# A gated mix of memory attention and a ReGLU network on one core: wq in row halves, ratios by GpSimd copies, another cut of the last tile, and a new order for late loads

## The chip, the cores and the metric

The kernel runs on one core of one Trainium2 chip. The metric is the device time of one execution in microseconds (us), from launch to end, the median of several runs. Engine names as in the profile: PE is TensorE (matmuls; PEld its weight loads), DVE is VectorE, ACT is ScalarE, POOL is GpSimd, SP is SyncE, which issues nearly all DMAs here.

## The reference

x is 2048 tokens by 512, in bfloat16. The output is `g * a + (1 - g) * b`, with one gate per token.

```python
g = _sigmoid((x * gate_w).sum(-1, keepdims=True))
# a: 32 heads of 16, 4 segments of 512 tokens
for s in range(N):
    logits = einsum('bhqd,bhkd->bhqk', qs, ks) * scale + mask     # causal within the segment
    a_dot = einsum('bhqk,bhkd->bhqd', softmax(logits), vs)
    num = einsum('bhld,bhde->bhle', phi(qs), M)                   # phi(t) = t + 1 if t > 0 else exp(t)
    den = einsum('bhld,bhd->bhl', phi(qs), z)[..., None] + 1e-06
    o = sig(beta) * num / den + (1 - sig(beta)) * a_dot
    M = M + einsum('bhld,bhle->bhde', phi(ks), vs)
    z = z + phi(ks).sum over tokens
a = o @ wo
# b: ReGLU with 1792 hidden columns
b = (relu(x @ W_gate) * (x @ W_up)) @ W_down
```

`q`, `k` and `v` are `x @ wq`, `x @ wk` and `x @ wv`.

## The kernel before

The work is cut into four segments of 512 tokens. For each, PE makes Q and K (heads on partitions, tokens on columns) and V, then for each of four groups of eight heads the scores, whose exponentials ACT writes to `E` tiles and POOL masks (L874, `affine_select`), then the product with V (PV, L896). DVE normalises that product (L927 to L932), turns it into `oT` (L908) and adds the recall from the memory of earlier segments (L912, L988). The network of the segment runs beside this: gate and up products, `rgr` on ACT (L1047), `hT` on DVE (L1053). The end of a segment is four output tiles of 128 tokens (`out_tile`), in which the down product of `hT` and the product of `oT` with `wo` accumulate in one PSUM bank; DVE scales it (L1075) and SP stores it. The very last tile is done in two halves of 256 columns.

PSUM has eight banks. Each product takes a bank and holds it until DVE or ACT has evicted it. So a late eviction holds up a later product on PE.

**Order.** All engines run lists that are fixed when the program is built. A planner, `Plan`, gets every piece of work as a task with an engine, a cost, dependences and a key, and lays the tasks out in time; the order in which it starts them becomes each engine's list. `LANDS` tells it when the first loads arrive, the last numbers in `plan.add` are the latencies it reckons with, and the table `SHIFT` moves the keys of some 1220 tasks one by one. At run time nothing of this is looked at: every engine runs its list in order and waits on semaphores. Where a load arrives later than planned, the engine that reads it waits, and with it all that stands behind in its list.

**PE's three modes.** Projections and the network use the whole array (`full`, L663) or, next to PV work, the same product as four column tiles of 32 (L667). Scores use row tiles (L823, L836), PV, denominators and memory use column tiles (L896, L952, L1002).

**The start.** Six dummy matmuls (L1090) come first. x of segment 0 comes as four tiles `xn` and is turned on PE (L699) into `xT[0]`; other segments are turned by a DMA (`load_xT`). The loads of weights go out in this order on SP: wq in two halves with the x tiles between (`load_q`), wk, wv, gate and up weights in pieces, down weights, wo. A half of wq is 256 of its 512 output columns, 512 bytes per row of wq. In `proj_q` the first two column groups of segment 0 are made in two halves of 256 tokens, and need only the first half of wq.

**Token gates.** `gate_tasks` multiplies `xn` with `gate_w` (L610, four per segment), and takes an exponential (L616), `rcol`. PE has no need of it, but three readers have: `ngcol` (L620, L621) scales the output, and the ratios in another layout scale the attention (`grc`, L653) and the recall. For segments 1 to 3 that layout comes from DMAs through DRAM (`ratio`, `rtok`, `rq`, `rr`; L637 to L648). For segment 0 it comes from a matmul with a fold of the identity:

```python
nc.vector.tensor_tensor(q0[:], rcol..., quad..., ALU.mult)          # L626
nc.tensor.matmul(bank(sl)[:, 0:16], lhsT=fold..., rhs=q0...)        # L629
nc.vector.tensor_tensor(grc..., src()..., gcat..., ALU.mult)        # L653
```

There is one buffer `xn`. The load for the next segment (`load_xn`, L480) waits for the four products of the segment before, and its own four products wait for it.

Of the kernel before, what the change touches and what calls it, by code (L numbers as in the profile page):

```python
# [35 lines left out]
    0: -25684, 1: 1407, 2: -1330, 3: -22978, 4: -30607, 6: 36389, 7: -5637, 8: -6641, 9:  # L36
    -9156, 10: 6383, 11: -4187, 12: -13726, 13: 12497, 14: 57538, 15: -5422, 16: 1476, 17:
    -21591, 18: 23771, 19: -4129, 20: -7981, 21: 280, 22: 7068, 25: -318, 28: 21268, 29:
    -15341, 30: -57736, 31: -21028, 32: -2196, 33: -8016, 34: -783, 35: -1107, 36: -633, 38:
    15, 40: 42372, 41: 65840, 42: 5113, 43: -71216, 44: 19414, 45: 21758, 47: 5746, 50: 654,  # L40
    51: 20403, 52: 53629, 53: -20631, 54: 7059, 55: -21405, 56: -13895, 57: -740, 58: -5913,
    59: -13897, 60: 1353, 61: -40120, 62: 24385, 63: -14621, 65: 25112, 66: 3543, 67: -38939,
    69: 6399, 71: -26793, 72: -4691, 73: -2524, 75: 40537, 76: -4748, 77: -586, 80: -1662, 81:
    -105183, 82: -62163, 83: -64288, 84: 18468, 85: -40339, 86: 37103, 87: -37065, 89: 8422,
    90: 16643, 91: -13637, 92: -14487, 93: -5073, 94: 1505, 96: -1554, 97: -747, 98: -9522,
    99: -4680, 100: 4639, 101: -97803, 102: 16395, 103: 38252, 104: -69147, 105: -10415, 106:
    27259, 107: -31419, 108: 13377, 109: -123574, 111: -12785, 112: -2378, 113: 3673, 114:
    -29140, 115: 4266, 116: -62363, 117: 88, 119: -4261, 121: -33231, 122: 9814, 123: 2110,
    125: 19178, 126: 17796, 127: -23382, 128: -6689, 129: -747, 130: 22411, 131: -31402, 132:
    -16511, 133: -1373, 134: -1496, 135: 8763, 136: 29491, 137: -749, 138: 29552, 139: -20100,  # L50
    140: 44658, 141: -80409, 142: -3139, 143: -26909, 144: 1803, 145: 386, 146: 16247, 147:
    65537, 148: -3529, 149: -6241, 150: 65653, 151: 46999, 153: 14030, 154: 44020, 155: 14760,
    156: 43561, 157: -7096, 158: 45936, 159: -26024, 160: 23457, 161: 50979, 162: -46625, 163:
    -54482, 164: 88981, 165: -28687, 166: -9744, 167: 114272, 168: -31967, 169: 9267, 170:
    38917, 171: -13229, 172: 5693, 173: -28492, 174: 3768, 177: 340, 178: -26186, 179: -31211,
    181: -31531, 182: 39351, 183: -15341, 184: -100921, 185: 22252, 186: -1779, 187: -3708,
    189: -4467, 191: 37936, 192: -46874, 193: 73026, 194: -5245, 196: 16791, 197: 4743, 198:
    -45159, 199: -43211, 200: -20335, 201: 1213, 202: 125, 203: 797, 204: 8260, 205: -173671,
    206: -2254, 207: 2086, 208: -44938, 209: 42530, 210: 2685, 211: -40581, 212: 31594, 213:
    -29665, 214: -2192, 215: -61393, 217: 4901, 218: 62, 219: -31560, 220: 8015, 221: -19756,  # L60
    222: -10130, 223: -18144, 224: 68794, 225: -54104, 226: -17099, 227: 38555, 228: 53992,
    229: -20805, 230: 2476, 231: -36425, 232: -2988, 233: -4667, 234: -11209, 235: 1392, 236:
    -22096, 237: -41776, 238: -415, 239: 1533, 240: 386, 241: 10244, 242: 16354, 243: -68385,
    244: 1929, 245: -59988, 246: -4306, 247: -23793, 248: -103183, 249: -2675, 250: 35079,
    251: 580, 253: -493674, 254: -20933, 255: 697, 256: -72948, 257: -3646, 258: -15000, 259:
    2471, 260: -20761, 261: -743, 262: 7412, 263: 20962, 264: 1114, 265: -5477, 266: 29635,
    267: -95694, 268: 15975, 269: -918, 270: -11522, 271: -41685, 272: 41485, 274: -239341,
    275: -1143, 276: -1006, 277: -1966, 278: -1511, 279: -68031, 280: 21386, 281: 115009, 283:
    -13976, 285: -26218, 286: 8903, 287: 24823, 288: 3414, 289: 51471, 290: 44714, 291: 65457,
    292: -5775, 293: 23342, 294: -52538, 295: 42735, 296: 28700, 297: -891, 298: 169, 299:  # L70
    -16564, 300: -37658, 301: 52198, 302: -77259, 303: 19215, 304: 4223, 305: 38165, 306:
    173397, 307: 2166, 308: 18393, 309: 36863, 310: 1124, 311: 3176, 312: 15683, 313: -68358,
    314: 1939, 315: -10804, 316: 34, 317: -980, 318: -3471, 320: -41264, 321: -2068, 323:
    1048, 324: -899, 325: -107092, 326: 2450, 328: 543, 329: 4991, 330: 2135, 331: 32862, 332:
    11444, 333: 4290, 334: 12303, 336: 16672, 337: -8199, 338: -10438, 340: 3207, 341: 19188,
    342: 51335, 344: 41704, 345: 8287, 346: -7332, 347: 9844, 348: 72410, 349: -2946, 350:
    -4692, 351: -51689, 352: 139925, 353: 1013, 354: 37165, 355: -35242, 356: -37552, 357:
    40840, 358: -57531, 360: 338, 361: 34813, 362: -9340, 363: 15621, 365: 7805, 366: 167,
    367: -28467, 368: 3566, 369: 1686, 370: 32158, 371: -28595, 372: -13605, 373: -620, 374:
    -29762, 375: -50578, 376: -29094, 377: -4500, 378: -18438, 379: 6926, 380: -11713, 381:  # L80
    2592, 382: 28678, 384: 25379, 385: 31823, 386: 16340, 387: 17046, 388: 60789, 389: -730,
    390: 4582, 391: -15468, 392: 66683, 393: 43214, 394: 11631, 395: -22092, 396: 26488, 397:
    -65824, 398: 51325, 399: 4073, 400: 417, 401: -12246, 402: 2493, 403: 60686, 404: 33157,
    405: -9018, 406: -3996, 407: -134963, 408: -21328, 409: 1451, 410: 7686, 411: -1030, 412:
    -27724, 413: 18333, 414: 11330, 415: 8620, 416: -71493, 417: 7355, 418: 51598, 419: -8421,
    420: 7069, 421: 3185, 422: -36336, 423: 87360, 424: -6430, 425: 16914, 426: 11785, 427:
    62686, 428: 52403, 429: -14143, 430: -4565, 431: 4777, 432: -31918, 433: 11745, 434:
    10666, 435: 94, 436: 686, 437: 25603, 438: 17039, 439: -1226, 440: 1265, 441: -20575, 442:
    8235, 443: -3138, 444: -30408, 445: 5091, 446: 19491, 447: -54497, 448: -22163, 449:
    -49529, 450: 45855, 451: 6110, 452: -2600, 453: 27760, 454: 7956, 456: 14632, 457: 14498,  # L90
    458: -7407, 459: 246, 460: 54389, 461: -45592, 462: -12249, 463: 9152, 464: 7024, 465:
    8349, 466: 8939, 467: -12828, 468: -5305, 469: -28674, 470: 1790, 471: 22067, 472: 8119,
    473: 5003, 474: 1424, 475: -40794, 476: 1452, 477: 120749, 478: 4568, 480: -35928, 481:
    -5506, 482: 61504, 483: 34766, 484: -8966, 485: -17563, 487: 29633, 488: 6458, 490: 15043,
    491: 7030, 492: -15797, 493: 25921, 494: 17134, 495: 360, 496: 34064, 498: -3554, 499:
    1864, 500: -3887, 501: 59696, 502: -2935, 503: -60651, 504: -42594, 505: 213, 506: -17474,
    507: -2187, 508: 95, 509: -34011, 510: -1408, 511: 5879, 512: -203909, 513: 73486, 514:
    28663, 515: 10250, 517: 10912, 518: 10294, 520: 57556, 521: 46448, 522: 7685, 523: -830,
    524: 25912, 525: -41304, 526: 78731, 527: 56834, 528: 2389, 529: 6987, 530: -8151, 531:
    7296, 532: 457, 533: 40865, 534: 9213, 535: -7140, 536: 1038, 537: 3375, 539: -30525, 540:  # L100
    17951, 541: 3198, 542: -28519, 543: -67, 544: -8718, 545: 21976, 546: 1952, 547: 3138,
    548: -58497, 549: 38416, 550: 22607, 551: 172585, 552: 30409, 553: 19609, 554: -59594,
    555: 18272, 556: 63244, 557: 51613, 558: 18778, 560: 1285, 561: 8777, 562: 859, 563:
    64816, 564: 10753, 565: 5534, 566: 27513, 567: -666, 568: 42956, 569: -32272, 570: -2400,
    571: -34879, 572: 28274, 573: -45032, 574: 7638, 575: 1838, 576: 6680, 577: 20107, 578:
    14616, 579: -4332, 580: -28208, 581: -14633, 582: 734, 584: -32958, 585: -2694, 586: 2834,
    587: -9046, 588: 2913, 589: 46788, 590: -11636, 591: -1009, 593: -21251, 594: 3643, 596:
    -27878, 597: -2270, 598: -1189, 599: 4132, 600: 1971, 601: 56415, 602: 5034, 603: -36,
    604: 569, 605: 7285, 606: 3301, 607: -30637, 608: 6437, 609: -1424, 610: -20036, 611:
    5297, 612: 1078, 613: -2111, 614: 5218, 615: 2106, 616: 20150, 617: -65962, 618: 14301,  # L110
# [272 lines left out]
def kernel(  # L383
# [560 lines left out]
    def dens(seg, half):  # L944
# [17 lines left out]
        def dn():  # L962
            return dnr[ds.i][:]
# [195 lines left out]
```

## Time and profile before

| | |
|---|---|
| three runs | 266.34, 267.81, 267.84 us; median 267.81 |
| profiled execution | 269.25 us, of which the span from first to last instruction is 267.5 |
| PE busy | 257.2 us, 96% of the span, 3669 recorded matmuls |
| DVE, ACT, POOL busy | 198.7, 182.5, 57.8 us |
| granted TensorE clock | 1.000 |

The page divides the span into 40 slices of 6.7 us and gives each engine's busy share in tenths. PE's ends are modelled, so its rows are read by their starts. A wait is put down to what came last. Some matmul records are missing from a trace, so that a row may say x1 where two were run.

### The profile page before, as it was taken

How to read it: one execution, taken by the hardware profiler on the slowest of the kernel's cores; microseconds unless marked ns; L12 is line 12 of the kernel's file. 1: busy time of each engine (PE TensorE's matmuls, PEld its weight loads, DVE VectorE, ACT ScalarE, POOL GpSimd, SP SyncE). 2: the span in 40 equal slices, each digit the busy share in tenths (PEclk: the TensorE clock that was granted, in tenths of full speed). 3: DMA queues.
4: the chain of work that ended last, by engine and by line, in shares of the span. 5: the costliest groups of instructions: out<-in, count | busy, mean ns of one | idle time of the engine just before them, and what ended most of it. 6: DMA issues, size and time to landing. Idle time of an engine off the chain costs nothing.

```text
span 267.5 us, 8524 instructions
## 1 busy us (share of the span) xinstructions
PE 257.2 (96%) x3669; PEld 120.1 (45%) x3699; DVE 198.7 (74%) x455; ACT 182.5 (68%) x168; POOL 57.8 (22%) x146
## 2 busy tenths in 40 slices
PE   8999999999998799999999999999999999999995
PEld 5444444445444244454544344534444444444554
DVE  4797889999794999896786998769782846536722
ACT  3269989999788387998498766798878786124000
POOL 7013142222321222222112231232132312000000
PEclk9999999999999999999999999999999999999999
DMA  7999981215039101200221012002200130000001
GB/s 216 349 250 341 248 191 28 86 29 104 20 66 210 36 12 35 89 14 11 45 73 51 22 23 102 30 0 56 82 2 0 32 100 22 20 0 0 5 22 61
DMA packets 32573, 20.62 MB, mean 77 GB/s; under 512 B 15000, under 2 KB 31000, under 8 KB 32536
## 3 DMA queue, kind: packets, MB, share of 16 engines
q1 hardware_dynamic: 32248, 19.82, 28.3%
q8 instruction: 29, 0.48, 0.7%
q10 hardware_dynamic: 288, 0.26, 0.3%
q14 instruction: 8, 0.07, 0.1%
HBM read 13.21 MB, written 2.55 MB: 59 GB/s over the span
## 4 chain that ended last, share of the span: by engine, by line
PE 79%; DMA 7%; DVE 5%; SPq 3%; ACT 3%; issue 2%; POOL 0%; DVEq 0%; ACTq 0%
PE ps L663 48%; PE ps L667 16%; PE ps L823 7%; PE ps L896 6%; DMA xn<-in_A_x_dram 3%; DMA wg_sb<-in_B_W_gate_dram 3%; ACT E L845 2%; SPq L470 2%; DMA pK<-pkT 1%; DVE junk L610 1%; PE ps L836 1%; PE ps L1002 1%; SPq L807 1%; DVE T L927 1%; SPq L507 0%
## 5 line engine op out<-in xcount | busy, mean ns | idle before, releaser
L845 ACT ACTIVATE E<-ps 128x2048 bf16<-128x2048 f32 x64 | 120.1, 1876 | 29.6 <-PE ps L823 23.7
L874 POOL TENSOR_SCALAR_AFFINE_SELECT E<-E 128x256 bf16<-128x256 bf16 x128 | 53.1, 438 | 169.2 <-ACT E L845 169.2
L1053 DVE TENSOR_TENSOR hT<-ps,rgr 128x512 bf16<-128x512 f32 x56 | 38.1, 686 | 19.0 <-ACT rgr L1047 12.4
L663 PE MATMUL ps<-xT,wu_sb 128*128 128x512 bf16 x194 | 50.1, 380 | 0.7 <-issue 0.6
L1047 ACT ACTIVATE rgr<-ps 128x512 bf16<-128x512 f32 x56 | 33.0, 599 | 21.7 <-PE ps L663 16.7
L663 PE MATMUL ps<-xT,wg_sb 128*128 128x512 bf16 x172 | 46.4, 380 | 0.4 <-issue 0.2
L663 PE MATMUL ps<-wd_sb,hT 128*128 128x512 bf16 x135 | 33.5, 380 | 0.9 <-issue 0.8
L927 DVE STREAM_TRANSPOSE T<-ps 128x512 f32<-128x512 f32 x32 | 21.7, 703 | 12.6 <-PE ps L896 11.5
L663 PEld LDWEIGHTS <-wu_sb 128*128 128x128 bf16 x200 | 18.4, 98 | 22.5 <-issue 1.7
L663 PEld LDWEIGHTS <-wg_sb 128*128 128x128 bf16 x180 | 16.5, 98 | 21.0 <-issue 2.7
L823 PE MATMUL ps<-QT,KT 32*128 32x320 bf16 (+3 forms) x512 | 25.4, 273 | 0.4
L1075 DVE TENSOR_SCALAR osr<-ps,ngcol 128x512 bf16<-128x512 f32 (+1 forms) x17 | 12.0, 706 | 13.9 <-PE ps L667 8.9
L667 PE MATMUL ps<-wd_sb,hT 128*32 128x512 bf16 (+1 forms) x384 | 20.4, 348 | 0.0
L663 PEld LDWEIGHTS <-hT 128*128 128x128 bf16 x142 | 12.9, 98 | 16.2 <-issue 2.3
L823 PEld LDWEIGHTS <-KT 32*128 32x128 bf16 x512 | 7.7, 92 | 26.4 <-issue 26.1
L896 PE MATMUL ps<-E,Vp 128*17 128x320 bf16 (+3 forms) x512 | 18.9, 274 | 0.0
L845 ACT ACTIVATE Em<-ps 128x2048 bf16<-128x2048 f32 x8 | 15.0, 1877 | 2.2 <-PE ps L836 2.2
L663 PE MATMUL ps<-wv_sb,xT 128*128 128x512 bf16 x60 | 16.1, 379 | 0.0
L663 PE MATMUL ps<-xT,wk_sb 128*128 128x512 bf16 x53 | 14.4, 380 | 0.7 <-issue 0.3
L610 DVE SCALAR_TENSOR_TENSOR junk<-xn,gwb 128x512 bf16<-128x512 bf16 x16 | 11.0, 688 | 3.8 <-DMA xn<-in_A_x_dram 3.8
L768 DVE CAST ktr<-ps 128x512 bf16<-128x512 f32 x16 | 10.9, 681 | 2.6 <-PE ps L663 2.6
L667 PEld LDWEIGHTS <-hT 128*32 128x32 bf16 x384 | 9.9, 97 | 6.4
(105 smaller groups left out, 294.8 us busy)
## 6 DMA issues: line engine op xcount, KB each, us to landing
cdr<-coefs SPq DMA_DIRECT2D x12, 256.0 KB
out_dram<-osr SPq DMA_DIRECT2D x15, 128.0 KB
wd_sb<-in_B_W_down_dram SPq DMA_DIRECT2D x2, 896.0 KB
xn<-in_A_x_dram SPq DMA_DIRECT2D x3, 512.0 KB
Vm<-Vp SPq DMA_DIRECT2D x8, 144.0 KB
wg_sb<-in_B_W_gate_dram SPq DMA_DIRECT2D x2, 512.0 KB
wu_sb<-in_B_W_up_dram SPq DMA_DIRECT2D x2, 512.0 KB
wg_sb<-in_B_W_gate_dram SPq DMA_DIRECT2D x2, 384.0 KB
```

What stands on the lines that cost most here:

```text
L610: zs.append(plan.add("DVE", 690, key, lambda t=t: nc.vector.scalar_tensor_tensor(junk[:], xn[:, t, :], 1.0, gwb[:], ALU.mult, ALU.mult, ac ...
L663: nc.tensor.matmul(out, lhsT=lhsT, rhs=rhs, start=start, stop=stop)
L667: nc.tensor.matmul(out[r], lhsT=lhsT[:, r], rhs=rhs, start=start, stop=stop, tile_position=(0, 32 * j))
L768: d = plan.add("DVE", 600, key - RQK, lambda: nc.vector.tensor_copy(ktr[ks.i][:], bank(sl)), [a], DVL + 40, need=[ks], frees=[sl])
L823: nc.tensor.matmul(ps[:, j * L + o:j * L + o + L - q], lhsT=KT[i][rows, kb, 3 * r:3 * r + 2].rearrange("p h q -> p (h q)"), rhs=QT[i][rows ...
L845: last_exp[0] = [plan.add("ACT", 66 + 4 * L / 1.2, key, lambda: nc.scalar.activation(dst, ps[:, 0:4 * L], ACT.Exp, scale=SCALE), [a] + war ...
L874: nc.gpsimd.affine_select(out=m[:, :, o:o + HP], in_=m[:, :, o:o + HP], compare_op=ALU.is_ge, fill=0.0, base=HP, pattern=[[0, 4], [1, HP]] ...
L896: nc.tensor.matmul(bank(sl)[32 * j:32 * j + HW, q:q + w], lhsT=(Vp[i] if n < 4 else Vm)[:, kb, r, 4 * c + j, 0:HW], rhs=rhs, start=(n == 0 ...
L927: done.append(plan.add("DVE", 633, key - RL, lambda r=r, sl=sl: nc.vector.transpose(T[ts.i][:, r], bank(sl)), [a] + done, 75 if r else 0, ...
L1047: r = plan.add("ACT", 478, key - RL, lambda sl=gsl, rs=rs: nc.scalar.activation(rgr[rs.i][:], bank(sl), ACT.Relu), [g], ACL, frees=[gsl])
L1053: nc.vector.tensor_tensor(hT[hs1.i][:], bank(sl), rgr[rs.i][:], ALU.mult)),
L1075: b = plan.add("DVE", 95 + 1.12 * w, key - RL, lambda: nc.vector.tensor_scalar(osr[os.i][:, 0:w], bank(sl)[:, 0:w], ngcol[:, tt:tt + 1], N ...
```

## The change

- wq is loaded in halves of 256 of its 512 input rows, 1024 bytes per row. In `proj_q` all four column groups of segment 0 first add up the first two row chunks, in two halves of 256 tokens, and then, once the second half of wq has come, the other two.
- For segment 0 the fold matmul, `fold`, `quad` and `q0` are gone. Instead POOL copies `rcol` in 16 small copies (32 partitions by 4) to `rq[0]`, and the product `grc` reads `rq` as for the other segments.
- The last output tile is done in 384 and 128 columns instead of 256 and 256.
- The planner is told other arrival times and longer latencies for DMAs, and a new table `SHIFT` with offsets for its tasks (some 1220 entries, not shown); the lists of all engines change with it.

```diff
@@ LANDS
-    LANDS = dict(n0=3500, n1=3600, n2=4300, qa=5200, n3=5400, qb=6500, k=8250, v=9750, g0=11250,
-                 u0=12750, gw=13600, be=13800, g1=15150, u1=16550, x1=19850, g2=20950, u2=22150,
-                 g3=23350, u3=24550, d0=27400, d1=30000, o=31450, x2=33200)
+    LANDS = dict(n0=3500, n1=3600, n2=4300, qa=4900, n3=5400, qb=6100, k=8000, v=9500, g0=11100,
+                 u0=12700, gw=13400, be=13700, g1=15100, u1=16600, x1=19850, g2=21500, u2=22700,
+                 g3=23900, u3=25100, d0=28000, d1=30600, o=32000, x2=35300)
@@ load_q
-        return load_cols(nc.sync, wq_sb, A_wq, 256 * i, 256 * i + 256, "q" + "ab"[i])
+        return load(nc.sync, wq_sb[:, 2 * i:2 * i + 2, :],
+                    A_wq.rearrange("(c p) n -> p c n", p=P)[:, 2 * i:2 * i + 2, :], "q" + "ab"[i])
@@ gate_tasks
-        if seg == 0:
-            sl, q0 = work(), sb([P, 4, 4], F32, "q0")
-            d = plan.add("DVE", 90, key, lambda: nc.vector.tensor_tensor(
...
-            d = plan.add("PE", 260, key, lambda: nc.tensor.matmul(
...
+        def spread(b):
+            for j in range(4):
+                nc.gpsimd.tensor_copy(rq[0][32 * j:32 * j + 32, b], rcol[32 * b:32 * b + 32, 0, 0:4])
+        if not seg:
+            d = [plan.add("POOL", 300, key, lambda b=b: spread(b), [c], POL) for b in range(4)]
@@ proj_q
-        if seg == 0 and c < 2:
+        if seg == 0:
             a = None
             for h in range(2):
-                a = matmuls(key + 20000 * (h - 1), [got_q[0]], sl, [
+                a = matmuls(K(-8 + h, c), [got_q[0]], sl, [
                     lambda ci=ci, h=h: (wq_sb[:, ci, c * P:(c + 1) * P],
                                         xT[0][:, ci, h * L // 2:(h + 1) * L // 2])
-                    for ci in range(NC)], width=L // 2, at=h * L // 2, prev=a,
-                    chunk={ci: got_x[0][ci // 2] if h else x0_first for ci in range(NC)})
+                    for ci in range(2)], width=L // 2, at=h * L // 2, prev=a, start=not h, stop=False,
+                    chunk={0: got_x[0][0] if h else x0_first})
+            a = matmuls(K(-6, c), [got_q[1]] + got_x[0][1], sl, proj_mm(wq_sb, c, 0)[2:], prev=a,
+                        start=False)
@@ latencies that the planner reckons with (from, to)
-   ratio 1500, rq 2200, rtok 1500, rr 2200, pK 1450, Vm 2800, coefs 2000, cdr 3000, out 1400, xn 3200, xT 2600
+   ratio 2500, rq 3500, rtok 2500, rr 3500, pK 3000, Vm 4300, coefs 2900, cdr 4200, out 2400, xn 6500, xT 4500
@@ ffn_tasks
-            for n0, n1 in [(0, D // 2), (D // 2, D)] if tt == NT - 1 else [(0, D)]:
+            for n0, n1 in [(0, 3 * P), (3 * P, D)] if tt == NT - 1 else [(0, D)]:
```

## The prediction

> **What bounds the kernel now.** I read the page's head first, for which engine fills the span.
>
> ```profile
> span 267.5 us, 8524 instructions
> PE 257.2 (96%) x3669; PEld 120.1 (45%) x3699; DVE 198.7 (74%) x455; ACT 182.5 (68%) x168; POOL 57.8 (22%) x146
> PE   8999999999998799999999999999999999999995
> ```
>
> TensorE (PE) is the bound: 96% busy, and at nines in every slice but the first, the two from 86.9 us (8 and 7) and the last. Other engines gain or lose time only where they make PE wait. The granted clock is 1.00 throughout, so a 512-column matmul costs the 0.216 us between starts that the trace shows in undisturbed stretches (28.33 to 29.20: four matmuls). Next, the waits of PE and of DVE (VectorE) between 76 and 92 us:
>
> ```profile
> PE ps L667 <- DVE Vp L798: 1.9, 1, 1.9
> PE ps L663 <- DVE omr L988: 0.2, 1, 0.2
> ```
>
> ```profile
> DVE junk L610 <- DMA xn<-in_A_x_dram: 3.6, 1, 3.6
> ```
>
> The long PE wait has a DVE instruction as its releaser, and DVE had itself stood still for a load. The chain of waits, in order of time, joins the two:
>
> ```profile
> 78.75 7.67 DMA xn<-in_A_x_dram
> ...
> 86.44 0.70 DVE junk L610 x2
> 87.14 0.10 DVE rp L620
> ...
> 87.53 0.57 DVE Vp L798
> ```
>
> The load of `xn` for segment 3 takes 7.67 us. The first gate product (L610) waits for it, and the eviction `Vp` (L798), which needs nothing of that load, waits behind it in DVE's queue. The timeline of PE shows the price:
>
> ```profile
> 85.99 0.29 PE L896 MATMUL ps<-Em,Vm 128*17 128x64 bf16 x16
> 88.16 0.40 PE L667 MATMUL ps<-pqT,mbd 128*32 128x512 bf16 x4 [1.88 <-DVE Vp L798]
> ...
> 90.12 0.38 PE L663 MATMUL ps<-pqT,mbd 128*128 128x512 bf16 x1
> 90.70 0.59 PE L663 MATMUL ps<-xT,wq_sb 128*128 128x512 bf16 x2 [0.20 <-DVE omr L988]
> ```
>
> First 1.88 us, then one matmul at 90.12 is followed after 0.58 instead of 0.216: 0.36 more. Together 2.24 us, the only large hole after the start.
>
> **The change part by part.** The PE work is the same: equal multiplications, sometimes as one 128-wide matmul, sometimes as four 32-wide ones side by side at the same 0.216. The sum is therefore made of holes and small extras.
>
> *Order for late loads.* In the changed order the third `xn` load (L481 there) goes out right after segment 2's last product, as before, but 19 DVE instructions stand between that product and segment 3's first one, where 9 stood. By the spacings of their rows (0.65 for an `osr`, 0.60 for casts and products, 0.63 for transposes, 0.1 to 0.35 for the small ones) the nineteen fill about 7.4 us without any wait of DVE's own; the nine filled 4.1. On the SP queue the load now has two output stores and small ratio transfers near it; the two 256 KB `cdr` loads that were issued 2 us behind it come later. The trace's other two `xn` loads landed 4.0 and 3.3 us after their start. So even a load as slow as 7.67 is nearly covered: −2.24, between −1.9 and −2.3. What is late next: other DMA chains (`coefs` to `cdr`, `pkT` to `pK`) get larger latencies in the plan, which puts their readers later; I count nothing for them.
>
> *Ratios by GpSimd copies.* Removed from PE is the fold matmul, fp32 in two passes:
>
> ```profile
> 26.45 0.29 PE L629 MATMUL ps<-q,fold 128*128 128x16 f32 x2
> 26.59 0.59 PE L663 MATMUL ps<-xT,wk_sb 128*128 128x512 bf16 x2
> ```
>
> It held PE for 0.14 us: −0.14. The removed DVE setup (L554 to L560, under 1 us before 2.6 us) stood ahead of a DVE that idled until 4.25: nothing.
>
> Added are 16 copies of 32 partitions by 4 elements on POOL (GpSimd), and a wait: the gate product on DVE (L639) needs all of them. In POOL's queue twelve stand ahead of the third score tile's two masks and four behind. Behind the gate product on DVE stand a `KT` product and the eviction `Vp` (L786) that frees a bank for PE. Call a copy c, and T the end of the exponential `rcol` that they read. The bank is free at T + 16c + 0.85 (two masks, at 415 ns) + 0.2 (handoffs) + 0.37 + 0.26 + 0.69 (gate, `KT`, `Vp`) + 0.15 (handoff) = T + 16c + 2.5. T itself comes about 2.35 after the third score group: 0.4 of ACT's earlier work, 1.88 for the score exponential, 0.1. From that group to the matmul that needs the bank PE has 28 full matmuls and a score group with two mode changes: 6.05 + 0.33 + 0.2 = 6.6, so it arrives at T + 4.2. The stall is 16c − 1.7 us where that is positive. No POOL copy is in the trace. The nearest rows:
>
> ```profile
> L874 POOL TENSOR_SCALAR_AFFINE_SELECT E<-E 128x256 bf16<-128x256 bf16 x128 | 53.1, 438 | 169.2 <-ACT E L845 169.2
> L545 POOL TENSOR_SCALAR_AFFINE_SELECT tri<-tri 64x64 bf16<-64x64 bf16 x2 | 0.5, 234 | 0.1
> L1143 POOL MEMSET const-float32-0.0<- 128x1 f32 x1 | 0.1, 98 | 0.3 <-issue 0.3
> ```
>
> Least: the four L1143 memsets start 34 ns apart, 0.54 for sixteen: no stall. Most: the two L545 selections start 280 ns apart: 4.5, a stall of 2.8. In between, the undisturbed 415 for 256 elements and 234 for 64 leave about 176 for 4; successive masks start 48 ns before the one ahead has ended, so c = 0.128. That row reads and writes as a copy does, so I take it: +0.35, ends 0 and +2.8. The masks come up to 2 us later; their readers, the first PV group, stand some 50 matmuls behind: covered.
>
> The Trainium skill speaks against this move. "GPSIMD Engine Reference", section 3.1, gives about 156 ns for DVE's dispatch of an instruction and two software hops for GpSimd's; with 156 as a floor for c the stall is an estimated 0.8, and the forecast would be 266.3 instead of 265.8. The trace's own memsets, 34 ns apart, are below that floor, but they read nothing.
>
> *wq in row halves.* Packets of 512 bytes become 1024. DMA moves 294 GB/s between 3.0 and 5.5 us, while wq loads, and 367 between 6.5 and 9.0, while wk does. 512 KB at those rates is 1.78 and 1.43; the packet records (27 ns and 46 ns on 16 engines) say 1.73 and 1.47. So `wk` lands some 0.26 earlier than now, when PE waits for it:
>
> ```profile
> 6.31 2.12 PE L663 MATMUL ps<-xT,wq_sb 128*128 128x256 bf16 x14
> 8.73 1.25 PE L663 MATMUL ps<-xT,wk_sb 128*128 128x512 bf16 x5 [0.30 <-DMA wk_sb<-in_A_wk_dram]
> ```
>
> But the new order has two 256-column matmuls, 0.22, fewer ahead of the first K matmul, so the hole stays: −0.04 (0 to −0.35). The first score group comes after 36 full-array matmuls of Q, K, V and gate instead of 56; ACT starts early, and PE gains nothing by it.
>
> *Last tile as 384 and 128.* What follows the last matmul is its eviction: 736 ns for 512 columns, 484 for 256, so about 0.35 for 128: −0.13. The 384 columns' eviction (0.62) hides under the 18 steps of the other part, 18 × 0.054 = 0.97. If the loading of weights showed at 128 columns (the full-array L699 steps of that width start 0.106 apart), it would be +0.94; the 34-column steps L1002, four tiles each, take 0.037 (64 matmuls in 0.60), loads included, so I take 0.
>
> *Mode changes.* PE switches between full array, row tiles and column tiles 145 times before, 147 after; one costs 0.095 (at 25.25, a score group starts 0.53 after the last pair instead of 0.43): +0.19.
>
> Sum: −2.24 − 0.14 − 0.13 − 0.04 + 0.35 + 0.19 = −2.0 us. The profiled execution took 269.25 (its span 267.5 and 1.75 around it), so 267.25; it lies 1.4 above the median of the runs, 267.81, and I carry the difference over: **265.8**.
>
> **The rivals.** *The copies eat the gain*: c between 0.2 and 0.28, DVE waits and PE stalls 1.5 to 2.8: 267 to 268.2. For: POOL's masks vary from 409 to 972 ns, so it can be disturbed. Against: the copies hold only 4 elements.
>
> *The xn hole is not in the plain runs*: the lowest run, 266.34, is 1.5 under the median, about the size of the hole. If the median has none, what is left is +0.2: 268.0. Against: the load's neighbours are the same in every run.
>
> *Slower*: GpSimd copies that cross partitions cost as much as a whole mask, 0.415. Then 16c − 1.7 = 4.9, and −2.35 + 4.9 gives 270.4. It decides from c = 0.27, where the gain is gone. Against: the tri row's 234 for 64 elements.
>
> *The holes close entirely*: no stall from the copies and smaller waits gone too: 265.0 or less.
>
> **How the numbers follow.** The forecast 0.5, its own range 265.1 to 266.6; holes closed entirely 0.26; copies eat the gain 0.1; no hole in the plain runs 0.08; slower by the copies or by a wait that the new order brings 0.06. The range 264.2 to 268.2 leaves out the last and the extremes. A measurement of this kernel tells about 1% (2.7 us) from no change: under 265.13 is faster, over 270.49 slower. Faster: nearly all of "closed entirely" and a tenth of the forecast, 0.31; slower 0.05; within 0.64.
>
> **What would show it.** PE's wait at L667 for `Vp` gone and DVE's wait for `xn` under 1 us; 16 POOL rows `rq<-rcol` near 20 us with mean near 0.13 to 0.18; DVE waiting at L639 for POOL about a microsecond, PE under 0.5 behind it; `wk` landing near 8.4; the last eviction near 0.35. A PE wait over 1.5 us anywhere after 9 us makes the prediction wrong; so does an `xn` wait that only moved.

## The result: 268.95 us, half a per cent slower, and the profile after

The changed kernel took 268.95 us, the median of 11 runs (268.58 to 270.02). The kernel before, run beside it, took 267.66 (11 runs, 266.33 to 268.15). The ratio is 1.006, with an interval from 1.0041 to 1.008: slower, by less than 1%. The forecast was 265.8 with a range up to 268.2.

The profiled execution took 268.58 us. In the head of its page the 8 and the 7 of the two slices from 80.3 to 93.6 us (the prediction put them at 86.9) have become nines, and a 7 stands in the fourth slice, 20.0 to 26.7 us.

```profile
span 266.9 us, 8279 instructions
PE 256.9 (96%) x3543; PEld 118.3 (44%) x3574; DVE 197.9 (74%) x447; ACT 182.4 (68%) x168; POOL 60.5 (23%) x162
PE   7997999999999999999999999999999999999994
```

31 of the 3574 matmul records are missing, so "PE busy" is a little too low, and only the waits that have a releaser are read here. From the view of waits, one of PE's and one of DVE's:

```profile
PE ps L649 <- DVE Vp L786: 1.4, 1, 1.4
```

```profile
DVE grc L639 <- POOL rq L619: 2.4, 1, 2.4
```

The wait of 1.9 us at 86 us is gone, and DVE no longer waits for `xn` there. The new wait sits where the prediction put it. The timeline shows POOL, then DVE, then PE (start, duration, what; in brackets the idle time ahead of it and its releaser):

```profile
20.56 2.61 POOL L619 COPY rq<-rcol 32x4 f32<-32x4 f32 x12 [1.86 <-ACT rcol L609]
23.24 0.78 POOL L862 TENSOR_SCALAR_AFFINE_SELECT E<-E 128x256 bf16<-128x256 bf16 x2
24.08 0.84 POOL L619 COPY rq<-rcol 32x4 f32<-32x4 f32 x4
```

```profile
24.95 0.37 DVE L639 TENSOR_TENSOR grc<-rq,gcat 128x128 f32<-128x128 f32 x1 [2.42 <-POOL rq L619]
25.24 0.46 DVE L759 TENSOR_SCALAR KT<-ktr,mcol_o 128x512 bf16<-128x512 bf16 x1
25.62 0.67 DVE L786 CAST Vp<-ps 128x512 bf16<-128x512 f32 x1
```

```profile
23.94 1.03 PE L649 MATMUL ps<-wv_sb,xT 128*128 128x512 bf16 x4
26.35 0.59 PE L649 MATMUL ps<-xT,wg_sb 128*128 128x512 bf16 x2 [1.38 <-DVE Vp L786]
```

Twelve copies, two masks, four copies; then the gate product, one `KT` product and the eviction `Vp`. PE's four matmuls from 23.94 would have been followed at 24.80; the next came at 26.35, a stall of 1.55. PE stands still once more, for 0.2, ahead of its matmul at 27.88, until the next `Vp` (27.14 to 27.82) is done. The group of the copies gives one copy:

```profile
L619 POOL COPY rq<-rcol 32x4 f32<-32x4 f32 x16 | 2.9, 180 | 2.5 <-ACT rcol L609 1.9
```

A copy takes 180 ns, but twelve of them fill 2.61 us: they start 0.22 apart.

At the start, the first K matmul comes at 8.59 instead of 8.73. The end is longer. DVE's last eviction and SP's last store, in the kernel before and in the changed one:

```profile
264.53 0.48 DVE L1075 TENSOR_SCALAR osr<-ps,ngcol 128x256 bf16<-128x256 f32 x1 [1.48 <-PE ps L667]
265.04 0.33 SPq L1078 DMA_DIRECT2D out_dram<-osr  x1
```

```profile
263.37 0.35 DVE L1063 TENSOR_SCALAR osr<-ps,ngcol 128x128 bf16<-128x128 f32 x1 [0.39 <-PE ps L653]
263.75 1.03 SPq L1066 DMA_DIRECT2D out_dram<-osr  x1
```

The eviction shrank to 0.35 as reckoned, but the issue of the store that follows takes 1.03 us instead of 0.33. From the end of the last eviction to the end of the span it was 2.5 us (265.01 to 267.5) and is now 3.2 (263.72 to 266.9).

### The profile page after: what moved, and what is told of

It is laid out like the page before. It is cut to its first block, busy times and chain, and to the rows that moved or that the text cites. A ratio compares the mean times of both kernels' runs of the same rounds, so it can differ in the third digit from the quotient of the medians.

```text
span 266.9 us, 8279 instructions
## 1 busy us (share of the span) xinstructions
PE 256.9 (96%) x3543; PEld 118.3 (44%) x3574; DVE 197.9 (74%) x447; ACT 182.4 (68%) x168; POOL 60.5 (23%) x162
## 4 chain that ended last, share of the span: by engine, by line
PE 88%; issue 3%; ACT 3%; DMA 2%; POOL 1%; DVE 1%; SPq 1%; ACTq 0%; POOLq 0%; DVEq 0%
PE ps L649 58%; PE ps L653 13%; PE ps L811 8%; PE ps L884 7%; DMA wk_sb<-in_A_wk_dram 2%; ACT E L833 2%; POOL rq L619 1%; PE ps L824 1%; PE ps L990 1%; SPq L471 1%; DVE Vp L786 0%; ACT rgr L1035 0%; POOL E L862 0%; PE ps L940 0%; ACT ex L718 0%
## 5 line engine op out<-in xcount | busy, mean ns | idle before, releaser
L649 PE MATMUL ps<-xT,wg_sb 128*128 128x512 bf16 x203 | 53.0, 380 | 1.9 <-DVE Vp L786 1.4
L1035 ACT ACTIVATE rgr<-ps 128x512 bf16<-128x512 f32 x56 | 32.4, 599 | 15.4 <-PE ps L649 12.7
L649 PE MATMUL ps<-wd_sb,hT 128*128 128x512 bf16 x141 | 35.9, 380 | 0.9 <-issue 0.8
L649 PEld LDWEIGHTS <-wg_sb 128*128 128x128 bf16 x210 | 19.7, 98 | 25.5 <-issue 3.4
L1063 DVE TENSOR_SCALAR osr<-ps,ngcol 128x512 bf16<-128x512 f32 (+2 forms) x17 | 12.0, 706 | 13.0 <-PE ps L653 8.3
L653 PE MATMUL ps<-wd_sb,hT 128*32 128x512 bf16 (+2 forms) x360 | 18.2, 346 | 0.0
L649 PE MATMUL ps<-xT,wq_sb 128*128 128x512 bf16 (+1 forms) x64 | 15.1, 353 | 0.3 <-issue 0.2
L649 PE MATMUL ps<-wv_sb,xT 128*128 128x512 bf16 x58 | 15.2, 380 | 0.1
L844 DVE TENSOR_TENSOR Em<-Em,tri 128x1024 bf16<-128x1024 bf16 x16 | 10.6, 685 | 4.1 <-ACT Em L833 4.1
L718 ACT ACTIVATE ex<-QT 128x512 bf16<-128x512 bf16 x12 | 7.6, 632 | 7.6 <-DVE QT L740 7.6
```

The costliest lines, as they stand in the source:

```text
L649: nc.tensor.matmul(out, lhsT=lhsT, rhs=rhs, start=start, stop=stop)
L653: nc.tensor.matmul(out[r], lhsT=lhsT[:, r], rhs=rhs, start=start, stop=stop, tile_position=(0, 32 * j))
L718: return es, plan.add("ACT", 520, key + 500, lambda: nc.scalar.activation(ex1[es.i][:], src(), ACT.Exp), [a], ACL, need=[es])
L844: att["diag", u + v] = plan.add("DVE", 605, key, lambda v=v: nc.vector.tensor_tensor(Em[:, :, v], Em[:, :, v], tri[:, None, None, :].to_br ...
L1035: r = plan.add("ACT", 478, key - RL, lambda sl=gsl, rs=rs: nc.scalar.activation(rgr[rs.i][:], bank(sl), ACT.Relu), [g], ACL, frees=[gsl])
L1063: b = plan.add("DVE", 95 + 1.12 * w, key - RL, lambda: nc.vector.tensor_scalar(osr[os.i][:, 0:w], bank(sl)[:, 0:w], ngcol[:, tt:tt + 1], N ...
```

## The experiments

Differences between kernels are differences of medians. The experiments ran in four groups on three chips, each group beside its own runs of the kernel before (medians 267.60, 267.40, 267.14 from a single run, and 268.00), so a difference between kernels of two groups can be off by some tenths. "Side by side" below means that two traces are compared at the same weight load of PE, of which no record is missing; this shows where in the kernel a difference comes about.

**Four copies instead of sixteen.**

```diff
-            for j in range(4):
-                nc.gpsimd.tensor_copy(rq[0][32 * j:32 * j + 32, b], rcol[32 * b:32 * b + 32, 0, 0:4])
+            nc.gpsimd.tensor_copy(rq[0][32 * b:32 * b + 32, b], rcol[32 * b:32 * b + 32, 0, 0:4])
```

> The changed kernel with 4 GpSimd copies instead of 16; the other 12 blocks of rq hold zeros, so the attention of segment 0 is scaled by wrong ratios; every list but GpSimd's is the same. Theory (the copies hold up VectorE's gate product, and TensorE 1.4 to 1.6 us behind it; the hole of the xn load is absent from most plain runs of the kernel before): VectorE's wait at the gate falls from 2.42 to under 0.3 us, TensorE's 1.38 us wait for Vp at 26 us is gone, and the time falls from 268.95 to 267.3 - 267.6, a ratio of 0.998 to 1.000 to before. Rival 1 (the new order costs time elsewhere, the copies little): it stays above 268.5. Rival 2 (the hole is in the plain runs of before and was removed, something else of over 2 us was added): the same wait goes, and the time is 267.5 as well, so it is told apart by the run with the small xn load.

A memset that sets `rq[0]` to zero at the start belongs to the edit too. Measured: 267.21 us (12 runs, 266.56 to 268.21), ratio to before 0.9964 (0.9938 to 0.999), 1.74 less than the changed kernel. DVE's wait for POOL is gone, and of PE's waits between 9 and 40 us one is left:

```profile
PE ps L649 <- DMA wk_sb<-in_A_wk_dram: 0.7, 1, 0.7
```

So twelve copies cost 1.74 us. Side by side, the two profiles part by 1.77 us, all of it between 24.5 and 28 us: the stall of 1.55 and the 0.2 behind it.

**Thirty-two copies.**

```diff
             for j in range(4):
-                nc.gpsimd.tensor_copy(rq[0][32 * j:32 * j + 32, b], rcol[32 * b:32 * b + 32, 0, 0:4])
+                for _ in range(2):
+                    nc.gpsimd.tensor_copy(rq[0][32 * j:32 * j + 32, b], rcol[32 * b:32 * b + 32, 0, 0:4])
```

> The changed kernel with every GpSimd copy made twice, 32 in all. Theory: 16 more at 0.221 us from start to start make the gate product 3.5 us later, and nothing on TensorE covers any of it now: 268.95 + 3.5 = 272.5, ratio 1.018. Rival 1 (the copies are covered in plain runs): under 270.5.

Measured: 275.54 us (4 runs), ratio 1.0287 (1.0233 to 1.0342): 6.6 more than the changed kernel. PE's wait, and the granted clock in the 40 slices:

```profile
PE ps L650 <- DVE Vp L787: 5.3, 1, 5.3
PEclk9999599999999999999999999999999999999999
```

The wait grew by 3.9, as sixteen more copies at 0.22 should make it (3.5). The rest is a surprise. The slice from 27.4 to 34.2 us has half the clock; in the windows view the mean clock is 0.79 between 20 and 36 us. The trace's record of the clock has the half from 28.14 to 34.97: it begins 3.3 us after PE's last matmul ahead of the wait had ended (24.8) and lasts 4.9 us beyond the wait (30.09). In those 4.9 us PE's matmuls start 0.43 apart, so about 2.4 us are lost. The tail, from the last eviction to the end, is 0.7 longer than in the changed kernel, which the last experiments take up. The kernels with a stall of 1.4 show full clock there.

**The third load of xn made small**, in the kernel before.

```diff
-        nc.sync.dma_start(out=xn[:], in_=x[seg * L:(seg + 1) * L, :].rearrange(
+        w = 32 if seg == 3 else D
+        nc.sync.dma_start(out=xn[:, :, 0:w], in_=x[seg * L:(seg + 1) * L, 0:w].rearrange(
```

> The kernel before, with the xn load of segment 3 cut to 32 of 512 columns (the gates of segment 3 are then made mostly from segment 2's tokens); all lists are the same. Its wait of 3.58 us on VectorE and the 1.88 us behind it on TensorE go in any case. Theory (the hole is absent from most plain runs): the median falls by under 0.7 us, ratio 0.997 to 1.000. Rival 2 (the hole is in the plain runs as in the profile): it falls by 1.9 to 2.3 us to about 265.5, ratio 0.992.

**The kernel before, once more.** No edit; one profiled execution.

> The kernel before, profiled once more. Theory: TensorE's wait for Vp between 76 and 92 us is under 0.7 us this time, and the profiled execution takes 267.0 to 267.9. Rival 2: the wait is 1.5 to 2 us again.

Measured: the small load gives 267.10 us (12 runs, 266.44 to 267.58), ratio 0.9974 (0.9948 to 0.9999), 0.5 less than the kernel before beside it. The second profile of the unchanged kernel took 267.31 us, not 269.25. Its window from 76 to 92 us (the second number is PE's busy time), first in the profile that the prediction was made from, then in the second one, and DVE's wait in the second one:

```profile
76.00:92.00 16.00, 13.58 (x190) 6.08 (x192) 12.08 (x31) 11.27 (x10) 3.25 (x9) 1.00 0.49 102
```

```profile
76.00:92.00 16.00, 16.00 (x210) 6.81 (x209) 15.13 (x38) 12.44 (x12) 3.97 (x10) 1.00 0.53 110
```

```profile
DVE junk L610 <- DMA xn<-in_A_x_dram: 0.5, 1, 0.5
```

Same program, same load, a wait of 0.5 on DVE instead of 3.6, and no hole on PE. Side by side, PE is 0.4 to 0.6 us later in the second profile from the first K matmul to 86 us, and 1.96 earlier from 92 us to the end: the hole and the start are the whole difference, and the hole is 2.6 us by this reckoning. The profile with the small load differs from the second one by 0.02 at the end.

The hole belongs to some executions and not to others. The landings show where the two profiles part. A load is spread over 16 DMA engines and lands in 16 parts. Fifteen parts of this one had landed by 82.31 and the last at 86.42; in the second profile by 82.98 and at 84.00. In both, packets of 256 bytes, by size and time those of the transposing load `pK` (L784), are held on several engines, from 83.81 to 86.39 and from 84.53 to 87.08. The late part came ahead of that in the second profile and only with its end in the first. That this makes the hole was not tried.

The plain runs say how often something like it happens: of the 74 runs of the kernel before in the four timed comparisons, 17 lie above 268.5 us, 7 of them among the 23 beside which the small load ran; its own 12 are all below 267.6. That those 17 have this very hole is likely and not shown, as only two of the executions were profiled.

**The gate product late, and the last tile cut as before**, each alone and both together. The first edit puts the gate product of segment 0 right ahead of its first reader; only DVE's list changes.

```diff
     order = plan.run()
+    gate = att["gate", 0]
+    order.remove(gate)
+    first = next(n for n, t in enumerate(order) if any(d is gate for d, _ in t.deps))
+    order.insert(first, gate)
```

```diff
-            for n0, n1 in [(0, 3 * P), (3 * P, D)] if tt == NT - 1 else [(0, D)]:
+            for n0, n1 in [(0, D // 2), (D // 2, D)] if tt == NT - 1 else [(0, D)]:
```

> Changed kernel with all 16 copies, but segment 0's gate product stands in DVE's queue right ahead of its first reader, behind the evictions that it held up; the output is complete. Theory (the copies cost only through DVE's queue: the eviction Vp waits behind the gate product): POOL's 16 copies still end near 24.9 us, the PE wait for Vp near 25 us is gone, PE busy in 9 to 36 us is 26.4 or more as with four copies, and the time is 267.2, ratio to before 0.996. Rival (the copies themselves, or the later masks, cost): still a PE wait over 1 us somewhere in 9 to 36 us, 268.5 to 269, ratio 1.004.

> Changed kernel with the last tile cut 256 and 256 as before; the output is complete. Theory (the last store of 128 columns takes SP 1.03 us to issue where 256 columns took 0.33, more than the eviction saves): from the last matmul to the end of the span 3.35 instead of 3.8 us, time 268.5, 0.4 less than the changed kernel's 268.95. Rival (the prediction's term: the cut 384 and 128 saves 0.13): 269.1.

> Both edits: gate product late in DVE's queue and the last tile cut 256 and 256; the output is complete. If the two effects are independent: 268.95 - 1.7 - 0.45 = 266.8, ratio to before 0.997, with 0.14 of that from the fold matmul and 0.5 from the third xn load. Rival (the waits behind it only move): 267.5 or more, no faster than before.

| kernel | median (12 runs) | ratio to before | against the changed kernel |
|---|---|---|---|
| gate product late | 267.16 | 0.9982 (0.9962 to 1.0001) | −1.79 |
| cut 256 and 256 | 268.27 | 1.0015 (0.999 to 1.004) | −0.68 |
| both | 266.67 | 0.9969 (0.9947 to 0.9991) | −2.28 |

With the gate product late, POOL is as slow as ever and `Vp` no longer waits for it. The timeline of POOL, of DVE and of PE:

```profile
24.37 0.97 POOL L619 COPY rq<-rcol 32x4 f32<-32x4 f32 x4
```

```profile
22.75 0.68 DVE L786 CAST Vp<-ps 128x512 bf16<-128x512 f32 x1
```

```profile
24.00 1.03 PE L649 MATMUL ps<-wv_sb,xT 128*128 128x512 bf16 x4
24.87 0.59 PE L649 MATMUL ps<-xT,wg_sb 128*128 128x512 bf16 x2
```

The last four copies end at 25.34, after which the gate product could run; `Vp` ran at 22.75, and PE goes on after 0.87, four matmuls, without a wait. The whole cost of the copies was the place of one waiting instruction in DVE's queue. The later masks and the copies themselves cost nothing that shows.

The old cut gives back 0.68, or 0.49 where the gate product is late. In the profiles the tail, from the end of the last eviction to the end of the span, is 2.5 with the old cut in both kernels, as before, where it is 3.2 and 3.4 with the new one; side by side the end comes 0.5 and 0.8 earlier. (The two profiled executions took 268.70 and 267.32 us all the same, because PE waited 0.8 and 0.6 for `wk` at their start.) The prediction's −0.13 has the wrong sign.

**Why the end is longer: other cuts.** Both on the kernel with the gate product late; 128 columns ahead of 384, and 320 ahead of 192.

```diff
-            for n0, n1 in [(0, 3 * P), (3 * P, D)] if tt == NT - 1 else [(0, D)]:
+            for n0, n1 in [(0, P), (P, D)] if tt == NT - 1 else [(0, D)]:
```

```diff
-            for n0, n1 in [(0, 3 * P), (3 * P, D)] if tt == NT - 1 else [(0, D)]:
+            for n0, n1 in [(0, 320), (320, D)] if tt == NT - 1 else [(0, D)]:
```

> The changed kernel with the gate product late, last tile cut 128 first and 384 last; the output is complete. Theory (a store with rows of 256 bytes holds SP long, wherever it stands): the 128-column store, now the last but one, takes SP 1.0 to 1.3 us, the 384-column store after it 0.33, and from the end of the last eviction to the end of the span it is 2.5 us as with 256 columns. Rival (the last store of the kernel is slow when another store has just gone out, or because it is the last): the 384-column store takes 1 us, the 128-column one 0.33, and the tail stays at 3.2 to 3.4.

> The changed kernel with the gate product late, last tile cut 320 and 192, so that the last store has rows of 384 bytes; the output is complete. If the time that SP needs grows with the shortness of the rows: between 0.33 and 1.03 us, tail after the last eviction between 2.5 and 3.2. If only rows under 512 bytes are slow, all alike: 1.0 to 1.3 us and 3.2 to 3.4. If only 256 bytes are: 0.33 and 2.5.

Measured, one execution each: 266.65 and 266.60 us. The 128-column store, now the last but one:

```profile
259.13 0.33 SPq L1066 DMA_DIRECT2D out_dram<-osr  x1
```

It takes 0.33, so a store with rows of 256 bytes is not slow by itself: the theory fell. The rival fell too, since the last store, of 384 columns, also took 0.33, and the tail was 2.6 (262.32 to 264.9). With 192 columns the issue took 0.33 and the tail 2.5, as if only rows of 256 bytes were slow, which the row above rules out. What sets the slow issues apart stands in the view of DMA queues. For the stretch from 261.8 to 263.0 us of the kernel with the gate product late and the cut 384 and 128 it lists (packets, MB, share of 16 engines):

```profile
q1 hardware_dynamic: 136, 0.09, 25.1%
q8 instruction: 1, 0.02, 5.8%
```

One packet of q8 "instruction": in the packet records it has 16,384 bytes and runs from 261.86 to 262.98, in the middle of the 384-column store. Nine tenths of that store's packets (38 ns each, by the median) had begun by 262.46; its last one ended at 263.61. SP's last issue begins at 262.03 and ends at 263.35, 0.37 after the instruction packet. In the changed kernel that packet runs from 263.48 to 264.44 and the issue from 263.75 to 264.78, 0.34 after it; with four copies to 263.80, and the issue to 264.17; with 32 copies to 270.87, and the issue, 1.45 us long, to 271.24. In the seven other profiles up to here the last issue took 0.33: five began after the packet, two in its last 0.3 us. The kernel before has 29 such packets, the changed one 28; their 3699 and 3574 matmuls with as many weight loads are 28.9 and 27.9 times 256 instructions. The Trainium skill states the size: "Runtime: NRT & Kernel Launch", section "Instruction fetch mechanics", has engines refill their instructions in blocks of 16 KiB, 256 instructions, at a cost that it calls mostly hidden. The trace agrees on the size and the number; here the block isn't hidden.

**The block moved.** 60 more PE instructions ahead of everything, the cut 384 and 128 kept.

```diff
-        for k in range(6):
-            nc.tensor.matmul(bank(warm[k % 8]), lhsT=junk[:, 0:P],
-                             rhs=junk[:, None, 0:P].to_broadcast([P, 4, P]), start=True,
-                             stop=True)
+        for k in range(36):
+            nc.tensor.matmul(bank(warm[k % 8])[0:32, 0:96], lhsT=junk[:, 0:32],
+                             rhs=junk[:, 0:96], start=True, stop=True)
```

> The changed kernel with the gate product late and the cut 384 and 128 kept; the 6 warm-up matmuls of 512 columns at the start become 36 of 96 columns with 32-column weights, which are 60 more PE instructions ahead of everything else; the output is complete. Theory (SP's slow last issue is a collision with the load of a 16 KB block of instructions, whose place follows the number of PE's instructions): in the tail 256 PE instructions take 4.8 us, so the block comes 1.1 us earlier, about 260.7 to 261.9 us instead of 261.86 to 262.98; the last store's issue takes 0.33 us instead of 1.32, the tail after the last eviction is 2.6 instead of 3.4, and the time 266.5. Rival (the cut 384 and 128 is slow by itself, two stores 0.74 us apart): issue 1.0 to 1.3, tail 3.2 to 3.4, time 267.2. If the smaller warm-up lowers the granted clock at the start, that shows before 9 us and is counted apart.

Measured: 266.33 us (8 runs, 266.25 to 268.16), ratio 0.994 (0.9906 to 0.9975). The packet moved by 0.81 us, to 261.05 to 262.09. SP's last issue with the block in its old place and in the new:

```profile
262.03 1.32 SPq L1066 DMA_DIRECT2D out_dram<-osr  x1
```

```profile
261.97 0.49 SPq L1066 DMA_DIRECT2D out_dram<-osr  x1
```

The issue again ends 0.37 after the packet, which now costs little; the tail is 2.6 (261.94 to 264.5) instead of 3.4, and the median is 0.83 lower, on another chip. The last eviction starts at the same place (261.59, was 261.65), so the gain is in the tail. The cut of 384 and 128 isn't slow; it was unlucky in where it fell: side by side this kernel ends 0.05 ahead of the one with both edits above, with 0.16 of waiting still in the issue. Both are faster than the kernel before, by 0.6 and 0.3% (0.994 and 0.9969, intervals below 1), and than the changed one; the moved block and the gate product's place together are worth 2.6 us on the changed kernel.

## Why the prediction was wrong

It named the right places, and sized three terms wrongly, all towards a gain.

**The hole at 76 to 92 us: carried to runs that don't have it.** The mechanism was right as far as it shows: in the changed kernel the load goes out at 83.50 and its first reader runs at 92.53, 9.0 us later, so that even a load of 7.67 would have been covered, and none of the nine profiles with the new order has the wait. But of the two profiles of the kernel before, one has it and one hasn't, and the step "it lies 1.4 above the median of the runs, and I carry the difference over" took the hole of 2.24 off a median that hardly had it. The profiled execution was above the median because of the hole. On the median its removal is worth 0.5. That one step is off by 1.7 us. The rival "the xn hole is not in the plain runs" was in the main this case; it was given 0.08, although all three runs shown lay 1.4 or more below the profiled execution. "The load's neighbours are the same in every run" was true and beside the point: the same load with the same neighbours made DVE wait 3.6 us once and 0.5 the other time.

**The copies: c was 0.221, not 0.128.** The row was well chosen: 176 ns were estimated for a copy and 180 were measured. What failed is the subtraction after it: masks start 48 ns before the one ahead has ended, copies 41 ns after. Sixteen times 0.09 is 1.5 us. The formula 16c − 1.7 gives 1.84 at 0.221; the profile shows 1.55 and 0.2 behind it, the experiments 1.74 and 1.79, so the chain of masks, gate product, `KT`, `Vp` was right within 0.1. The floor that the prediction made of the Trainium skill's 156 ns ("GPSIMD Engine Reference", section 3.1) erred in the same direction, but less: 0.8 against 0.35. The rival "the copies eat the gain" had the right c and the right stall, and was set against a hole that it supposed to be filled.

**The last tile: −0.13 was +0.5 to +0.8.** The eviction shrank as worked out. The step took everything after it as fixed, and it isn't: SP's issue of the last store and the landing of the one ahead met a block of instructions. Nothing in the sum looked past the eviction. (The 0.106 between full-array steps of 128 columns, weighed there as a sign of weight loading, is from the start, where the 512-column dummy matmuls also start 0.43 apart, twice the 0.216; the L699 steps after 5.6 us start 0.06 apart. PE was slower at the start; the trace's record of a clock of 1.00 begins at 5.3 us.)

**The rest.** What remains of the change without the copies' wait and with the old cut is the kernel with both edits: 0.73 below the kernel before, 0.5 of it the hole. The fold matmul, the `wq` halves and the mode changes are then worth about −0.2 together, where +0.01 was reckoned; the runs don't tell them apart. The profiles agree on the size: from the first K matmul to the start of the last eviction it is 252.99 there, and 253.24 and 253.15 in the two profiles of the old order without the hole. What the `wq` halves bring at the start isn't shown: K began at 8.59 in the changed kernel and at 8.73 in the kernel before, but over the profiles at 8.2 to 9.5 with the new order and at 8.7 to 9.4 with the old. No extra cost from the longer latencies in the plan shows. The terms as measured, −0.5, +1.8, +0.6 and −0.2, make +1.7; the medians of the result say +1.3.

The range failed because its cases were taken one at a time: "no hole in the plain runs" at 268.0 and "the copies eat the gain" up to 268.2 came about together, with the tail on top.

## What to carry to other kernels

A hole in one profile is priced against that execution; before it is taken off the median of other runs, see whether their spread says that they have it. An instruction that waits for a slow helper belongs in its engine's queue right ahead of its first reader: moving it was worth the whole 1.8 us, with the slow copies kept. Follow the end of a kernel to the last landing, not to the last computing instruction, and look there for transfers that aren't the program's own.

## What the runs showed of the hardware

- A POOL copy of 32 by 4 fp32 elements took 180 ns, and twelve in a row started 221 ns apart in the changed kernel, where masks of 256 elements overlap by 48 ns.
- In a PE wait of 5.3 us the granted clock fell to half 3.3 us after the last matmul and stayed there for 6.8 us, 4.9 of them beyond the wait; in waits of 1.4 to 1.9 us it stayed at 1.00.
- A DMA issue on SP, 0.33 us by itself, took up to 1.45 us when it began while a 16 KB instruction packet was under way, 0.74 us after the 384-column store's issue: in five kernels it ended 0.34 to 0.37 after that packet. A packet alone doesn't hold it: in the twelve profiles 27 store issues began inside such a packet with no other issue of SP in the 1.3 us ahead, the one behind the 320-column store among them, and all took 0.33 or 0.34. That the store just ahead is what is needed was not tried. That the blocks are PE's follows from their number and from the move by 60 more PE instructions, 0.81 us where 1.1 was reckoned; the count alone doesn't set the place, as with the cut 128 and 384 the last one came at 260.27.
- The same kind of packet lies inside the slow load of `xn` (79.85 to 81.63 us in the profile of before, 1.78 us long; 80.45 to 81.63, 1.18 long, in its second profile), and the last of the load's 16 parts landed 4.1 and 1.0 us after the other fifteen. That the packet delays it was not tried.
